# Shifts of a 32-head attention kernel in pieces on GpSimd, wherever VectorE's plan has room; a fuller TensorE tick

## The chip, the cores and the metric

The kernel runs on one core of one Trainium2 chip. Its metric is the device time of a launch in microseconds (us), the median of some runs. A core has five engines with queues of their own: TensorE (PE in the profile) multiplies matrices into PSUM, ScalarE (ACT) and VectorE (DVE) work on SBUF and PSUM, GpSimd (POOL) works on SBUF, and SyncE (SP) here issues the DMAs. Every engine takes its instructions in the order in which the program emits them, and waits at an instruction for semaphores that others raise.

## The reference

It is attention with normalised queries and keys, for 32 heads of 2048 positions and 20 features, in bf16:

```
qn = q / (jnp.sqrt((q * q).sum(axis=-1, keepdims=True)) + eps)
kn = k / (jnp.sqrt((k * k).sum(axis=-1, keepdims=True)) + eps)
logits = jnp.einsum('bhqd,bhkd->bhqk', qn, kn) * t[None, :, None, None]
attn = _softmax(logits, axis=-1)
return jnp.einsum('bhqk,bhkd->bhqd', attn, v)
```

Each head has 2048 x 2048 logits, and each logit needs an exponential: 134 million in all. The logits of normalised vectors times a temperature near 1 are small, so no maximum is taken off.

## The kernel before, in words

**Two ways to an exponential.** The keys of a head are cut into 16 row blocks of 128, the queries into four groups of 512 columns. A block against a group is a unit, a PSUM bank of 128 x 512. For most blocks ScalarE computes the exponential of the scores from PSUM (psA) into a ring in SBUF (p_ring), in waves of two and three units in turn (line 785). TensorE multiplies it with the values (vaug, which has a column of ones for the softmax's denominator) into psO (line 714). For the other blocks VectorE does it: `DVE_TILES` (line 378) says how many blocks of each head, 4 to 6. For such a block, a *tile* of four units, VectorE reads the scores from PSUM (psD) in two instructions of 1024 columns, multiplies and adds, and writes int16 (xt, line 831): the bits of an fp16 number near the exponential, whose mantissa is linear in the logit. To smooth this out, three *shifts* follow, each an addition of 256, 512 or 768 (`PHASES`) to the int16 numbers, into tiles ss (line 851). TensorE multiplies xt with vaug and each of the three shifted tiles with values scaled by the matching power of two (vph), and so adds up four approximations.

**Shifts on GpSimd.** `KDN` (line 386) says for each head how many tiles have their third shift (`PSH` = 2) done by GpSimd: two pieces of `PCH` = 512 words each, a word being two int16 numbers that are added as one int32 (line 857). In all 99 shifts, 198 pieces. GpSimd also scales values (vph, line 522), normalises queries and keys of heads 3 and later (qkn, line 589) and divides the output (o_stage, line 738).

**Preparation.** For each head q and k are loaded into qk_sb (one buffer a head, 8 in turn), VectorE squares them (sq, line 554) and sums 32 rows of 20 (rs_sum, line 556); six small instructions make the inverse root (lines 559 to 577). Heads 0, 1 and 2 are prepared alone, then heads in pairs: squares and sums for each head, the small instructions for both. A transposing DMA and ten more bring the result into the layouts of TensorE (qkT, qz, kR).

**The plan.** The order of all engines comes from a planner in the kernel (`Program`, lines 44 to 340), which runs while the program is built. Each piece of work is a `Task` with an engine, a duration, dependences and a priority (a due time in heads). `list_schedule` plays the engines forward and lets each take the ready task with the least priority. It writes down the order; the semaphore waits follow from it. For GpSimd there is `pool_fill` (line 182): whenever VectorE is given an instruction that reads PSUM or reduces (names t1, tr, su), it is the *span* under which GpSimd's instructions are to lie, and a task of GpSimd that has a length `win` is placed there if it ends at most `OVER` = 0.03 us after the span. It then gets an extra dependence, its *trigger*: the instruction of VectorE just before, or the one before that. So GpSimd starts with the read and not in the middle of a shift.

`schedule` repeats that plan in passes. Score matmuls can run with 32, 64 or 128 rows of the array (`modes`; the score of 20 features fits in 32), and matmuls of fewer rows run beside each other. After each pass it adds up the TensorE columns that end in each stretch of `TICK` = 3.41 us, each task by its weight, and where the sum is under `LOAD` = 3500 it moves score matmuls to more rows (heavy), and takes some back where there are many more.

**Buffers.** xt has `NX` = 4 buffers, each ss `NE` = 3. A buffer is used again when its readers are done.

Of the kernel before, what the change touches and what calls it, by code (L numbers as in the profile page):

```python
# [9 lines left out]
BF16 = mybir.dt.bfloat16  # L10
FP16 = mybir.dt.float16
# [19 lines left out]
class Task:  # L31
    __slots__ = ("eng", "fn", "dur", "deps", "pri", "name", "lat", "dma", "n", "users",
                 "start", "end", "seq", "inc", "cnt", "rows", "work", "modes", "win", "trig")

    def __init__(self, eng, name, fn, dur, deps, pri, lat=0.0, dma=None):
        self.eng, self.name, self.fn, self.dur = eng, name, fn, dur
        self.deps = [d for d in deps if d is not None]
        self.pri, self.lat, self.dma = pri, lat, dma
        self.inc, self.cnt = False, 0
        self.rows, self.work, self.modes = 128, 512.0, None  # L40
        self.win, self.trig = 0.0, None


class Program:
# [3 lines left out]
    SEM_LAT = {"PE": 0.20, "ACT": 0.17, "DVE": 0.14, "POOL": 0.15, "SP": 0.0}  # L48

    SWITCH = 0.5  # L50
    LIGHT = 9.0
    TICK = 3.41
    LOAD = 3500.0
    PASSES = 12
    FIRM = 4
    MARGIN = 300.0
# [3 lines left out]
    SPARE = 0.0  # L60
    DSL = 0.6
    HOLDA = 0.7
    HPE = 0.1
    HDV = 0.08
# [11 lines left out]
    def schedule(self):  # L76
# [49 lines left out]
        self.heavy = heavy  # L126
        for t in self.tasks:
            if t.trig is not None:
                t.deps.append(t.trig)
        return self.order  # L130

    def list_schedule(self):
        for t in self.tasks:
            t.users = []
            t.trig = None
        for i, t in enumerate(self.tasks):
# [45 lines left out]
        def pool_fill(now):  # L182

            n = 0
            while True:
# [9 lines left out]
                fit = [r for r in ready["POOL"] if r[2].win and at + r[2].win <= span[1] + self.OVER]  # L195
                if not fit:
                    return n
                x = min(fit)
                ready["POOL"].remove(x)
                heapq.heapify(ready["POOL"])  # L200
                t = x[2]
# [6 lines left out]
                leave(t, now)  # L208
                n += 1
# [133 lines left out]
def bass_standalone__qk_norm__prompt_kernel(  # L343
# [16 lines left out]
    NB = 8  # L360
# [3 lines left out]
    NX = 4  # L364
    NE = 3
    GD = 1
# [5 lines left out]
    SPREAD = 0.8  # L372
    FIRST = -7.0
    DLEAD = 0.8
# [3 lines left out]
    DVE_TILES = [4, 4, 4, 5, 5, 5, 5, 5, 4, 5, 5, 5, 5, 4, 5, 5, 5, 5, 5, 5, 4, 5, 5, 5, 5, 6, 5, 5, 5, 4, 4, 6]  # L378
    NDMAX = 6
    NPOOL, FPOOL = True, True  # L380
    SQPOOL = False
# [4 lines left out]
    KDN = (4, 5, 2, 4, 3, 2, 4, 4, 2, 2, 4, 3, 3, 3, 4, 2, 4, 3, 3, 4, 3, 3, 5, 2, 3, 5, 2, 4, 2, 3, 3, 2)  # L386
    ADUR, ALAT = 0.95, 6.5
    PSH = 2
    ASTEP, AOFF = 2, 0
    ACCN = (0, 0, 0, 0, 0, 0, 0, 0, 0, 0, 0, 0, 0, 0, 0, 0, 0, 0, 0, 0, 0, 0, 0, 0, 0, 0, 0, 0, 0, 0, 0, 0)  # L390
    NLAST = 1
    PCH, PRATE = 512, 0.00164
    SHP = 0.0

    with ExitStack() as es:  # L395
# [7 lines left out]
        two = sbuf("two", [128, 1], I32)  # L403
        cst = sbuf("cst", [128, 2048], I16)
        ident = sbuf("ident", [128, 128], BF16)
        qk_sb = [sbuf(f"qk_sb{i}", [128, 2 * R, D], BF16) for i in range(NB)]
        vaug = [sbuf(f"vaug{i}", [128, R, 32], BF16) for i in range(NV)]
        vph = [sbuf(f"vph{i}", [128, len(PHASES), NDMAX, 32], FP16) for i in range(NV)]
        sqs = [sbuf(f"sq{i}", [128, 2 * R, D], BF16) for i in range(2)]
        rs = {x: sbuf(f"rs_{x}", [128, 4 * R], F32) for x in ("sum", "u", "a", "b", "y", "r")}  # L410
# [6 lines left out]
        xt = [sbuf(f"xt{i}", [128, GD * 2048], I16) for i in range(NX)]  # L417
        ss = [[sbuf(f"ss{j}_{i}", [128, GD * 2048], I16) for i in range(NE)] for j in range(len(PHASES))]
# [14 lines left out]
        def memset(eng, ap, val, dur, pri):  # L433
            return add(eng, "z", lambda e, tk: e.memset(ap, val), dur, pri=pri)
# [24 lines left out]
        D_groups = [list(range(i, min(i + GD, len(D_tiles)))) for i in range(0, len(D_tiles), GD)]  # L459
# [10 lines left out]
        memset("POOL", two[:, :].bitcast(I16), PHASES[PSH], 0.1, -98)  # L470
        z_cst = memset("POOL", cst[:, :], PHASES[2], 0.3, -70)
# [22 lines left out]
        last_sum = []  # L494
# [3 lines left out]

        def add_loads(h):
            b, bv = h % NB, h % NV  # L500
            pri = h - LEAD - 0.5
            war = (norm[h - NB] if h >= NB else []) + ([lambda: [trn[max(0, h - 4)]]] if h >= EARLY else [])
            x = qk_sb[b]
# [24 lines left out]
        def add_prep(hs):  # L528
# [16 lines left out]
            for i, h in enumerate(hs):  # L545
                x = qk_sb[h % NB]
                sqb = sqs[h % 2]
                if SQPOOL and h > 2:
                    m = 2 * R // NCH
                    s1 = [pool("sq", lambda e, tk, x=x, sqb=sqb, j=j: e.tensor_tensor(  # L550
                        sqb[:, j:j + m, :], x[:, j:j + m, :], x[:, j:j + m, :], ALU.mult),
                        m * D * TTRATE, lds[h] + last_sum[-2:-1]) for j in range(0, 2 * R, m)]
                else:
                    s1 = [dv("sq", lambda e, tk, x=x, sqb=sqb: e.tensor_tensor(sqb[:, :, :], x[:, :, :], x[:, :, :], ALU.mult),  # L554
                          0.41, lds[h] + last_sum[-2:-1] + (q0[2:] if h == 1 else []))]
                sums.append(dv("sum", lambda e, tk, i=i, sqb=sqb: e.tensor_reduce(  # L556
                    rs["sum"][:, 2 * R * i:2 * R * (i + 1)], sqb[:, :, :], AXIS_X, ALU.add), 0.73, s1 + prep_last[0]))
                last_sum.append(sums[-1])
            c = dv("rs", lambda e, tk: e.tensor_scalar(  # L559
                rs["u"][:, 0:w].bitcast(I32), rs["sum"][:, 0:w].bitcast(I32), -0.5, RS_MAGIC, ALU.mult, ALU.add),  # L560
                0.075 + 0.03 * n, sums)
# [20 lines left out]
            for i, h in enumerate(hs):  # L582
                x, b = qk_sb[h % NB], h % NN
                war = [trn[h - NN]] + (q0 if h == NN else []) if h >= NN else [z_qkn[b]]
                if NPOOL and h > 2:
                    norm[h] = []
                    m = 2 * R // NCH
                    for j in range(0, 2 * R, m):
# [3 lines left out]
                            m * D * TTRATE + 0.25, [c] + war, due + SPREAD)  # L592
# [32 lines left out]
        def first_head(rinv):  # L625
            x = qk_sb[0]
# [128 lines left out]
        def add_wave(w):  # L755
# [24 lines left out]
            for h in hs:  # L780
# [6 lines left out]
                0.0633 + n / 1200.0, qks + war, w)  # L787
# [13 lines left out]
        dusers = {}  # L801

        def add_dgroup(jg):
            js = D_groups[jg]
            sx, se = jg % NX, jg % NE
            w = 2048 * len(js)
            old = lambda n, ring: dusers.get((n, jg - ring), [])
            t1s = []
            for i, j in enumerate(js):
# [3 lines left out]
                for k in range(0, NG, n1):  # L813
# [11 lines left out]
                    for g in gs:  # L825
# [4 lines left out]
                    o = 2048 * i + 512 * k  # L830
                    t1_prev[nchunk[0]] = add("DVE", f"t1.{j}.{k}", lambda e, tk, o=o, slot=slot: e.tensor_scalar(  # L831
                        xt[sx][:, o:o + W1], psD[:, slot * W1:slot * W1 + W1], X_MUL, X_ADD, ALU.mult, ALU.add),
                        0.067 + W1 / 960.0, [qk] + old("x", NX), due - 5)
                    t1s.append(t1_prev[nchunk[0]])
            x = xt[sx][:, 0:w]

            def dv(name, fn, dur, deps):
                return add("DVE", f"{name}{js[0]}", fn, 0.068 + dur * len(js), deps, due)
            sh = []
            h0, n0 = D_tiles[js[0]][0], js[0] - d0[D_tiles[js[0]][0]]  # L840
            nd0 = DVE_TILES[h0]
            order = [(n * ASTEP + AOFF) % nd0 if math.gcd(ASTEP, nd0) == 1 else n for n in range(nd0)]
            kind = order.index(n0)
            by_dma = jg >= 2 and h0 < H - NLAST and kind < ACCN[h0]
            by_pool = jg >= 2 and not by_dma and kind < ACCN[h0] + KDN[h0]
            for i in range(len(PHASES)):
                dst, war = ss[i][se], t1s + old(f"s{i}", NE)
                if i == 2 and by_dma:
                    sh.append(None)
                elif i != PSH or not by_pool:  # L850
                    sh.append([dv(f"s{i}.", lambda e, tk, i=i, dst=dst: e.tensor_scalar(  # L851
                        dst[:, 0:w], x, float(PHASES[i]), None, ALU.add), 0.533, war)])
                else:
                    sh.append([])
                    for c in range(0, w // 2, PCH):
                        n = min(PCH, w // 2 - c)
# [98 lines left out]
```

## Time and profile before

| | |
|---|---|
| Median of 3 runs | 665.07 us (664.13 to 665.85) |
| The profiled execution, its own time | 664.62 us |
| Its span, first to last instruction | 662.8 us |
| Granted TensorE clock, mean | 1.000 |
| GpSimd (POOL) | 369.7 us busy, 375 instructions |
| DMA, mean over the span | 55 GB/s |

The span is what the profile's sums are made against; 1.8 us of the execution lie around it. A row of the groups gives a line and an engine, the operation, what is written and read, the shape and the count; behind the bar stand busy time and the mean length of a record in ns; behind the second bar the idle time of the engine before these instructions, with what ended it. Records of ScalarE and VectorE reach over the start of the next instruction, by 0.08 to 0.09 us on VectorE, so that the length of a record is not the time for which its engine's queue is held. From the order in time this is seen as the distance from start to start.

### The profile page before, as it was taken

How to read it: one execution, taken by the hardware profiler on the slowest of the kernel's cores; microseconds unless marked ns; L12 is line 12 of the kernel's file. 1: busy time of each engine (PE TensorE's matmuls, PEld its weight loads, DVE VectorE, ACT ScalarE, POOL GpSimd, SP SyncE). 2: the span in 40 equal slices, each digit the busy share in tenths (PEclk: the TensorE clock that was granted, in tenths of full speed). 3: DMA queues.
4: the chain of work that ended last, by engine and by line, in shares of the span. 5: the costliest groups of instructions: out<-in, count | busy, mean ns of one | idle time of the engine just before them, and what ended most of it. 6: DMA issues, size and time to landing. Idle time of an engine off the chain costs nothing.

```text
span 662.8 us, 14627 instructions
## 1 busy us (share of the span) xinstructions
PE 579.4 (87%) x5949; PEld 163.2 (25%) x5971; DVE 655.2 (99%) x927; ACT 655.1 (99%) x582; POOL 369.7 (56%) x375
## 2 busy tenths in 40 slices
PE   7787989988898888898889898888989889988997
PEld 2222222222222222222222222222222222222222
DVE  9999999999999999999999999999999999999997
ACT  8999999999999999999999999999999999999997
POOL 3346565565654456655666556565675664554550
PEclk9999999999999999999999999999999999999999
DMA  5454524243242432513435250353514224032200
GB/s 64 64 80 81 66 43 80 30 74 48 53 75 31 82 35 59 70 20 84 43 73 65 48 80 10 75 62 65 67 28 79 37 53 73 3 77 35 54 7 11
DMA packets 196723, 36.24 MB, mean 55 GB/s; under 512 B 172592, under 2 KB 196656, under 8 KB 196656
## 3 DMA queue, kind: packets, MB, share of 16 engines
q1 hardware_dynamic: 196512, 35.22, 34.0%
q8 instruction: 47, 0.77, 0.5%
q14 instruction: 20, 0.16, 0.1%
q10 hardware_dynamic: 144, 0.08, 0.1%
HBM read 7.87 MB, written 2.62 MB: 16 GB/s over the span
## 4 chain that ended last, share of the span: by engine, by line
ACT 91%; DVE 6%; DMA 1%; issue 1%; PE 0%; SPq 0%; ACTq 0%
ACT p_ring L785 91%; DVE xt L831 3%; DVE ss L851 1%; DMA qkT<-qkn 1%; DVE rs_sum L556 0%; DMA qk_sb<-in_k_dram 0%; DVE rs_u L559 0%; DMA qz<-qkT 0%; DVE sq L554 0%; SPq L431 0%; DVE qz L665 0%; DVE oT L727 0%; ACTq L395 0%; DVE kx L673 0%; DVE o_stage L738 0%
## 5 line engine op out<-in xcount | busy, mean ns | idle before, releaser
L785 ACT ACTIVATE p_ring<-psA 128x1024 bf16<-128x1024 f32 (+1 forms) x573 | 647.7, 1402 | 1.5 <-PE psA L694 1.5
L831 DVE TENSOR_SCALAR xt<-psD 128x1024 int16<-128x1024 f32 x308 | 374.9, 1217 | 1.7 <-PE psD L694 0.7
L857 POOL TENSOR_TENSOR ss<-xt,two 128x512 int32<-128x512 int32 x198 | 250.8, 1267 | 171.6 <-DVE ss L851 79.5
L694 PE MATMUL psA<-qz,kR 32*128 32x512 bf16 (+2 forms) x1063 | 217.5, 385 | 47.0 <-ACT p_ring L785 42.4
L851 DVE TENSOR_SCALAR ss<-xt 128x2048 int16<-128x2048 int16 x363 | 243.2, 688 | 0.0
L714 PE MATMUL psO<-ss,vph 128*32 128x512 f16 x1848 | 171.2, 385 | 0.7 <-POOL ss L857 0.7
L714 PE MATMUL psO<-p_ring,vaug 128*32 128x512 bf16 x1432 | 132.2, 385 | 0.7 <-ACT p_ring L785 0.7
L694 PE MATMUL psA<-qz,qkT 32*128 32x512 bf16 (+2 forms) x354 | 115.4, 384 | 15.0 <-ACT p_ring L785 13.4
L694 PE MATMUL psD<-qz,kR 64*128 64x512 bf16 (+1 forms) x456 | 118.5, 385 | 9.5 <-DVE xt L831 6.5
L694 PEld LDWEIGHTS psA<-qz,kR 32*128 32x128 bf16 (+2 forms) x1074 | 52.9, 92 | 183.1 <-ACT p_ring L785 179.7
L522 POOL TENSOR_SCALAR vph<-vaug 128x160 f16<-128x160 bf16 (+2 forms) x96 | 37.1, 386 | 48.9 <-DVE ss L851 22.5
L589 POOL TENSOR_TENSOR qkn<-qk_sb,rs_r 128x640 bf16<-128x640 bf16 x29 | 47.8, 1647 | 28.0 <-DVE ss L851 13.6
L714 PEld LDWEIGHTS psO<-ss,vph 128*32 128x32 f16 x1848 | 44.4, 94 | 73.1 <-issue 56.1
L694 PE MATMUL psD<-qz,qkT 64*128 64x512 bf16 (+1 forms) x153 | 57.6, 385 | 3.8 <-DVE xt L831 3.3
L714 PE MATMUL psO<-xt,vaug 128*32 128x512 f16 x616 | 59.9, 384 | 0.0
L714 PEld LDWEIGHTS psO<-p_ring,vaug 128*32 128x32 bf16 x1432 | 35.0, 94 | 54.9 <-issue 46.0
L738 POOL TENSOR_TENSOR o_stage<-oT,rec 128x320 bf16<-128x320 f32 x30 | 29.3, 978 | 33.3 <-DVE rec L730 15.8
L694 PEld LDWEIGHTS psD<-qz,kR 64*128 64x128 bf16 (+1 forms) x462 | 28.9, 93 | 71.5 <-DVE xt L831 57.2
L694 PEld LDWEIGHTS psA<-qz,qkT 64*128 64x128 bf16 (+2 forms) x358 | 28.0, 92 | 61.7 <-ACT p_ring L785 59.6
L556 DVE TENSOR_REDUCE rs_sum<-sq 128x32 f32<-128x640 bf16 x32 | 26.0, 812 | 0.1
L727 DVE STREAM_TRANSPOSE oT<-psO 128x512 f32<-128x512 f32 x32 | 22.7, 709 | 2.0 <-PE psO L714 2.0
L714 PEld LDWEIGHTS psO<-xt,vaug 128*32 128x32 bf16 x616 | 15.9, 94 | 23.1 <-issue 19.2
(47 smaller groups left out, 92.0 us busy)
## 6 DMA issues: line engine op xcount, KB each, us to landing
kR<-qkT SPq DMA_DIRECT2D x62, 96.0 KB, 2.2
qz<-qkT SPq DMA_DIRECT2D x124, 32.0 KB, 1.8
kR<-qkT SPq DMA_DIRECT2D x62, 64.0 KB, 2.0
qk_sb<-in_k_dram SPq DMA_DIRECT2D x32, 80.0 KB, 2.5
vaug<-in_v_dram SPq DMA_DIRECT2D x32, 80.0 KB, 3.6
qk_sb<-in_q_dram SPq DMA_DIRECT2D x124, 20.0 KB, 2.6
out_dram<-o_stage SPq DMA_DIRECT2D x31, 80.0 KB, 2.3
kR<-qkT SPq DMA_DIRECT2D x62, 32.0 KB, 1.9
```

Source lines behind the costliest of these rows:

```text
L522: vsc[h] = [add("POOL", f"vs{h}", lambda e, tk, i=i: e.tensor_scalar(vph[bv][:, i, 0:nd, :], vaug[bv][:, R - nd:R, :], 2.0 ** (-PHASES[i] ...
L556: sums.append(dv("sum", lambda e, tk, i=i, sqb=sqb: e.tensor_reduce(rs["sum"][:, 2 * R * i:2 * R * (i + 1)], sqb[:, :, :], AXIS_X, ALU.add ...
L589: u = add("POOL", f"norm{h}", lambda e, tk, x=x, b=b, i=i, j=j: e.tensor_tensor(qkn[b][:, j:j + m, 0:D], x[:, j:j + m, :], bc(rs["r"][:, 2 ...
L694: return eng.matmul(dst, lhsT, mov, tile_position=(p0, 0))
L714: last = eng.matmul(psO[32 * g:32 * g + 32, :], w, rhs_of(g), start=start, stop=False, skip_group_check=True, tile_position=(0, 32 * g))
L727: trO[h] = add("DVE", f"tr{h}", lambda e, tk: e.transpose(oT[:, :, :].rearrange("p r d -> p (r d)"), psO[:, :]), 0.63, [lambda: pv_users[h ...
L738: fin[h] = add("POOL" if pool else "DVE", f"fin{h}", lambda e, tk: e.tensor_tensor(st, src, rb, ALU.mult), TTDUR if pool else 0.40, [rc] + ...
L785: act[w] = add("ACT", f"exp{w}", lambda e, tk: e.activation(p_ring[:, p0 * 512:p0 * 512 + n], psA[:, slot * WAVES[0] * 512:slot * WAVES[0] ...
L831: t1_prev[nchunk[0]] = add("DVE", f"t1.{j}.{k}", lambda e, tk, o=o, slot=slot: e.tensor_scalar(xt[sx][:, o:o + W1], psD[:, slot * W1:slot ...
L851: sh.append([dv(f"s{i}.", lambda e, tk, i=i, dst=dst: e.tensor_scalar(dst[:, 0:w], x, float(PHASES[i]), None, ALU.add), 0.533, war)])
L857: u = add("POOL", f"s{i}.{js[0]}.{c}", lambda e, tk, i=i, dst=dst, c=c, n=n: e.tensor_tensor(dst[:, 2 * c:2 * (c + n)].bitcast(I32), xt[sx ...
```

## The change

The shifts that go to GpSimd are no longer listed by head. Every shift of a tile (but those of the first two) is a VectorE task that also has a form for GpSimd, `alt`. When `pool_fill` finds no other task of GpSimd that fits, it takes the last-due shift from VectorE's ready ones, if VectorE has at least `KEEP` = 0.3 us of other work ready, and cuts off as many words as fit into what is left of the span, at least 128, in steps of 32. The rest waits for the next span. Such a shift becomes GpSimd's for good; its matmuls wait for all its pieces.

```diff
+    PRATE = 0.00164
+    KEEP = 0.3
+    RESTP = 0.3
...
+    def piece(self, words, fixed=0.02):
+        return fixed + words * self.PRATE
...
-                fit = [r for r in ready["POOL"] if r[2].win and at + r[2].win <= span[1] + self.OVER]
-                if not fit:
-                    return n
...
+                room = span[1] + self.OVER - at
+                fit = [r for r in ready["POOL"] if r[2].win and r[2].win <= room]
+                if fit:
...
+                else:
+                    cand = [r for r in ready["DVE"] if r[2].alt]
+                    if not cand or self.piece(128) > room or sum(r[2].dur for r in ready["DVE"]) < self.KEEP + cand[0][2].dur:
+                        return n
+                    x = max(cand)
+                    ready["DVE"].remove(x)
...
+                    t.parent, t.rem, t.seq = x[2], 1024, x[2].seq
+                    t.parent.eng = "POOL"
+                rest = None
+                if t.parent:
+                    f = t.parent
+                    m = min(t.rem, max(128, int((room - self.piece(0)) / self.piece(1, 0.0)) // 32 * 32))
+                    if 0 < t.rem - m < 128:
+                        m = t.rem - 128
+                    if t.rem > m:
+                        rest = Task("POOL", f.name, None, 0.0, [], t.pri)
...
+                f = add("DVE", f"s{i}.{js[0]}", lambda e, tk, i=i, dst=dst: e.tensor_scalar(
+                    dst[:, be:be + w], xt[0][:, bx:bx + w], float(PHASES[i]), None, ALU.add), 0.068 + w / 3840.0,
+                    t1s + [u for m in range(len(js)) for u in old(f"s{i}", m)], due)
+                if len(js) == 1 and jg >= 2:
+                    f.alt = lambda c, n, i=i, dst=dst: lambda e, tk: e.tensor_tensor(
```

In the same diff the preparation changes. From head 3 on GpSimd folds the squares, the first ten features of each row added to the last ten (fold, in fp32), and VectorE sums what is left; heads 5 and later come in pairs with one square and one sum for both, heads 3 and 4 singly. For this qk_sb is one tensor.

```diff
-        preps = [[h] for h in range(min(NSOLO, H))] + [list(range(h, min(h + 2, H))) for h in range(NSOLO, H, 2)]
+        preps = [[h] for h in range(min(NSOLO, H))] + [[3], [4]] + [list(range(h, min(h + NQ, H))) for h in range(NSOLO + 2, H, NQ)]
...
+            parts = [(i, min(2, n - i)) for i in range(0, n, 2)] if FUSE and hs[0] > 2 else [(i, 1) for i in range(n)]
...
+                        c2.append(pool("fold", lambda e, tk, a=a, k=k, at=at: e.tensor_tensor(
+                            at[k + 1][0][:, a:a + 2 * R, :], at[k][0][:, a:a + 2 * R, 0:at[k + 1][1]],
+                            at[k][0][:, a:a + 2 * R, at[k + 1][1]:2 * at[k + 1][1]], ALU.add),
```

The constants change too. `LOAD`, the columns asked of each tick, goes up with the room kept when some are taken back; the planner's delays are set anew; the rings grow; and the tiles are spread differently over the heads, 157 for 154 in all.

```diff
-    SEM_LAT = {"PE": 0.20, "ACT": 0.17, "DVE": 0.14, "POOL": 0.15, "SP": 0.0}
-
-    SWITCH = 0.5
+    SEM_LAT = {"PE": 0.20, "ACT": 0.30, "DVE": 0.14, "POOL": 0.15, "SP": 0.0}
+
+    SWITCH = 0.1
...
-    LOAD = 3500.0
-    PASSES = 12
-    FIRM = 4
-    MARGIN = 300.0
+    LOAD = 3550.0
+    PASSES = 16
+    FIRM = 8
+    MARGIN = 600.0
...
-    NX = 4
-    NE = 3
-    GD = 1
+    NX = 6
+    NE = 4
...
-    DVE_TILES = [4, 4, 4, 5, 5, 5, 5, 5, 4, 5, 5, 5, 5, 4, 5, 5, 5, 5, 5, 5, 4, 5, 5, 5, 5, 6, 5, 5, 5, 4, 4, 6]
+    DVE_TILES = [4, 4, 4, 5, 4, 5, 5, 5, 5, 5, 5, 5, 5, 5, 6, 5, 6, 5, 5, 5, 5, 3, 5, 5, 5, 4, 5, 6, 6, 5, 5, 5]
```

## The prediction

> **What bounds the kernel now.** I read the busy totals first, then the chain of waits, then the groups with shapes kept apart, then the order in time.
>
> ```profile
> PE 579.4 (87%) x5949; PEld 163.2 (25%) x5971; DVE 655.2 (99%) x927; ACT 655.1 (99%) x582; POOL 369.7 (56%) x375
> ...
> PEclk9999999999999999999999999999999999999999
> ...
> ACT 91%; DVE 6%; DMA 1%; issue 1%; PE 0%; SPq 0%; ACTq 0%
> ...
> 54.99 602.71 ACT p_ring L785 x533
> ```
>
> Two engines are full, but the chain names one: from 55 us to 657.7 us it runs through 533 exponentials on ScalarE with nothing between them. VectorE is the co-bound: 99% busy, and hardly idle before any of its work.
>
> ```profile
> L785 ACT ACTIVATE p_ring<-psA 128x1536 bf16<-128x1536 f32 x286 | 461.2, 1613 | 1.5 <-PE psA L694 1.5
> L831 DVE TENSOR_SCALAR xt<-psD 128x1024 int16<-128x1024 f32 x308 | 374.9, 1217 | 1.7 <-PE psD L694 0.7
> L785 ACT ACTIVATE p_ring<-psA 128x1024 bf16<-128x1024 f32 x287 | 342.1, 1192 | 0.0
> L857 POOL TENSOR_TENSOR ss<-xt,two 128x512 int32<-128x512 int32 x198 | 250.8, 1267 | 171.6 <-DVE ss L851 79.5 <-DVE xt L831 30.2 <-DVE sq L554 12.4
> L851 DVE TENSOR_SCALAR ss<-xt 128x2048 int16<-128x2048 int16 x363 | 243.2, 688 | 0.0
> ```
>
> Records of one engine overlap, so the mean of a record is not what an instruction costs its queue. I use the distance from start to start: in the order in time three shifts start at 296.07 and the next read at 297.87, so **a shift costs 0.60 us**; reads at 294.94 and the shift after it at 296.07 give **1.13 us a PSUM read**, 0.09 under its record. For ScalarE the chain gives 602.71 / 533 = 1.131 us per exponential; the two shapes differ by (1613 - 1192) = 421 ns, so 1.34 us for 1536 columns and 0.92 us for 1024. The engine's records start the first exponential at 9.39 us and end the last at 658.6 us. Its 649 us hold about 640 us of bare work (286 x 1.330 + 287 x 0.904, the median distances) and 9 us of small stalls.
>
> **ScalarE's part.** DVE_TILES sums to 154 before and 157 after. A tile is four units of 512 columns, so 12 units leave ScalarE. Counted in the two programs, 286 wide and 287 narrow exponentials become 284 and 284: 2 x 1.34 + 3 x 0.92 = **-5.4 us**, all on the chain.
>
> **VectorE's part**, at start-to-start distances:
> - Three more tiles: 6 more reads x 1.134 = +6.8 us.
> - Shifts kept on VectorE: 363 to 352 (157 x 3 = 471, less 119 that GpSimd takes; before 99). 11 x 0.60 = -6.6 us.
> - Row sums. Before, 32 reductions of 640 elements at 0.73 (start to start; record 812 ns) = 23.3 us. After, three stay as they are (2.2), three read a folded half (0.065 + 320 / 960 = 0.40 each, 1.2), and 13 take two folded heads at once, again 640 elements, 0.73 each (9.5): 12.9 us, so -10.4 us.
> - Squares: 32 x 0.40 = 12.8 us become 6 x 0.40 + 13 x 0.73 = 11.9 us, -0.9 us. Only the shared start (0.065) is saved.
> - One more set of the small root instructions, since heads 3 and 4 are prepared singly: +0.4 us.
>
> Sum: **-10.7 us**. VectorE's work at median distances is 650.5 us now, so about 640 us after, against 634 + 9 us on ScalarE. ScalarE stays the end; VectorE's reserve grows by 10.7 - 5.4 = 5.3 us. That reserve covers what is uncertain below.
>
> **GpSimd's part.** 198 pieces of 512 words become 334 pieces of 128 to 672 words (59 of 672, 49 of 160, 51 of 192, 29 of 128), 121,856 words for 101,376, and 29 folds come in. GpSimd is 56% busy, with waits for VectorE inside that. Does a piece fit under its read?
>
> ```profile
> 249.77 1.42 POOL L857 TENSOR_TENSOR ss<-xt,two 128x512 int32<-128x512 int32 x1 [4.83 <-DVE rs_r L571]
> 252.21 1.65 POOL L589 TENSOR_TENSOR qkn<-qk_sb,rs_r 128x640 bf16<-128x640 bf16 x1 [1.02 <-DVE ss L851]
> ...
> 249.61 0.69 DVE L851 TENSOR_SCALAR ss<-xt 128x2048 int16<-128x2048 int16 x1
> 250.21 1.22 DVE L831 TENSOR_SCALAR xt<-psD 128x1024 int16<-128x1024 f32 x1
> ...
> 252.64 1.23 DVE L831 TENSOR_SCALAR xt<-psD 128x1024 int16<-128x1024 f32 x1
> 253.78 0.69 DVE L851 TENSOR_SCALAR ss<-xt 128x2048 int16<-128x2048 int16 x1
> ...
> 561.94 0.77 DVE L851 TENSOR_SCALAR ss<-xt 128x2048 int16<-128x2048 int16 x1
> ```
>
> A 512-word piece with nothing in its way has a record of 1.04 us (that at 293.13). Here it starts under a shift, takes 1.42 and ends at 251.19: it stood still for 0.38 us, until the read was about to begin, and ended 0.15 us before the next VectorE instruction (251.34). The 640-element norm does the same, ends at 253.86, **0.08 us after** the next shift began (253.78), and that shift is no longer than others (0.69, next start 0.59 later). The shift at 561.94 began 0.22 us before a GpSimd piece ended (561.12 plus 1.04); its record is 0.77, 0.09 over the usual. So about 0.13 us of overrun is free, and beyond that it costs its own length.
>
> A 672-word piece is not in the trace. From the norm (1.27 net for 640) and o_stage (0.73 for 320) a word costs 1.7 ns, so 1.04 + 160 x 1.7 ns = 1.31 us, an overrun of some 0.12 us: just inside what is free. Bounds: 0 and 0.04 us x 59 = 2.4 us on VectorE; I take 0, since the norm is nearest. Small pieces: bounds 0 (a 160-element vph scaling, 0.32 us, sits under reads unnoticed) and 0.09 us, the one measured block, for each of 334, 30 us. I take 0, because the plan gives each piece only what is left of its read; the upper end is the rival on the slow side.
>
> **A rule that speaks against it.** The Trainium skill, "GPSIMD Engine Reference", section 4.1 "Engine selection", says to keep elementwise adds off GpSimd, about twice as slow for two inputs; its section 3.1 gives 4497 ns for 2048 elements, 2.2 ns each. By that figure 121,856 words would be 268 us, and planned at 1.64 ns a word they would overrun their reads by 68 us in all, mostly out of VectorE's time: well above 700 us. The row says 1.04 us for 512 with start included, 1.7 ns a word at the margin, and the slow add costs nothing while VectorE reads PSUM beside it. I go by the row.
>
> **TensorE.** Counted in the two programs, 98 matmuls into psA run at full height (128 rows) for 66 before: 16 more narrow waves, whose two matmuls then follow one another, some 0.2 us more each, +3.2 us of TensorE. A tile on VectorE has four output passes for one, so three tiles add 36 output matmuls, nine groups of four at 0.4 us or less. TensorE is 87% busy. By the 33 full-height waves of before, ScalarE is on average 7 ns late, less than after the light forms (10 to 23 ns), so I cost this at 0; if TensorE had no slack it would be 16 x 0.2 = 3 us. The Trainium skill, "TensorE: Matmul & The Clock Gate", Part 1, has the clock halve after about 3.4 us of too little activity. By that rule a fuller tick could gain; by the row the granted clock is full in all 40 slices, so there is nothing to get back, and I take 0.
>
> **New waits.** A row sum now waits for a fold on GpSimd, with everything on VectorE behind it. The fold is placed about three heads ahead of its use, and other VectorE work stands between; cost 0, at most one late fold of 0.73 us x 16. Shift matmuls wait for a last piece; behind them on TensorE stand the scores that ScalarE needs. Before, TensorE's loads waited for GpSimd twice, 1.2 us in all. Twice as many pieces: 0 to 2.4 us; I take 0. The rings xt and ss grow from 4 and 3 to 6 and 4 buffers, which eases it. Head 3's and 4's loads go later in SP's queue by one head; the start (to 55 us, where ScalarE lost about 2 us) may move by 1 us either way.
>
> **The sum.** 664.62 us of the profiled execution (span 662.8, 1.8 around it) less 5.4 is 659.2; against the median of 665.07 it is 659.7. I say **659.5 us**, 0.8% faster.
>
> **Rivals.**
> - *VectorE's reserve also clears ScalarE's stalls.* Of the 9 us some 7 are stalls of 0.1 to 0.3 us spread over the run. Half of them gone: 656. For: VectorE less full. Against: they follow TensorE's queue, which gets fuller. 0.14.
> - *Late pieces stall TensorE's queue.* Each of 119 GpSimd shifts holding it 0.05 us gives the 5.4 back: 664.5. 0.09.
> - *Pieces block VectorE (slower).* Place: the shift that follows a read with a piece under it. Price: the 0.09 us seen at 561.94. From 10.7 / 334 = 0.032 us a piece on, VectorE is as full as today and the kernel turns slower; at two pieces of three (223 x 0.09 = 20 us) it is 650.5 - 10.7 + 20 = 660 us of VectorE work, 9 over today: 674. For: the largest pieces stand at the edge. Against: 198 pieces and 29 norms almost never blocked. 0.15.
> - The forecast, 657 to 663: 0.62.
>
> A measurement of this kernel tells about 0.3% (2 us) from no change. The cases give faster 0.78, same 0.07, slower 0.15. The range from 655 to 666.5 leaves the blocked case out.
>
> **What would show it.** Right: the unbroken run of exponentials about 5 us shorter (597 us for 602.71), shifts still 0.60 us start to start, VectorE's share a point or two lower. Wrong: shift records well over 0.69 after reads with a 672-word piece; VectorE at 99% with longer records; "POOL ss" as the releaser of TensorE loads with more than a few us; a granted clock under 1.

## The result and the profile after

| | before | after |
|---|---|---|
| Median, measured side by side | 664.98 us (664.13 to 665.85, 4 runs) | 661.5 us (660.44 to 662.2, 4 runs) |
| Ratio, 95% interval | | 0.9946 [0.9926, 0.9967] |
| The profiled execution, its own time | 664.62 us | 662.08 us |
| Its span | 662.8 us | 660.4 us |
| Granted TensorE clock, mean | 1.000 | 0.995 |

The change makes the kernel 0.5% faster, 3.5 us. That is less than the 0.8% forecast, and more than the 0.3% that can be told from nothing. The page after has these busy totals, clock slices and shares of the chain of waits:

```profile
PE 591.1 (90%) x5979; PEld 168.0 (25%) x6007; DVE 645.3 (98%) x902; ACT 649.7 (98%) x577; POOL 469.2 (71%) x542
...
PEclk9999899999999999999999999999999999999999
...
ACT 81%; DVE 14%; PE 2%; SPq 1%; issue 1%; DMA 1%; POOL 0%; DVEq 0%
```

Three things are to be seen. GpSimd went from 56% to 71% busy, and VectorE from 655.2 us to 645.3 us: the work moved. ScalarE lost only 5.4 us of records and still is what the run ends with. And two places are new: the fifth clock slice (66 to 82.5 us) is under 9, where before all 40 were full, and the chain is on ScalarE for 81% instead of 91%: after the stretch described below it runs through VectorE, and the last unbroken run of exponentials begins only at 123.63 us:

```profile
123.63 532.56 ACT p_ring L849 x471
```

The groups, all shapes of a line together (busy and mean record in ns, then the idle time ahead and what ended it):

```profile
L849 ACT ACTIVATE p_ring<-psA 128x1024 bf16<-128x1024 f32 (+1 forms) x568 | 642.5, 1433 | 5.1 <-PE psA L758 5.0
L916 POOL TENSOR_TENSOR ss<-xt,add_w 128x672 int32<-128x672 int32 (+14 forms) x335 | 322.5, 969 | 110.5 <-DVE ss L912 58.0
L905 DVE TENSOR_SCALAR xt<-psD 128x1024 int16<-128x1024 f32 x314 | 381.9, 1216 | 9.2 <-PE psD L758 7.9
L912 DVE TENSOR_SCALAR ss<-xt 128x2048 int16<-128x2048 int16 x352 | 234.5, 681 | 0.3
```

The shift records are 681 ns for 688 before, so the pieces under the reads do not lengthen them. But ScalarE now waits 5.1 us for TensorE's scores where it waited 1.5 us, and VectorE 9.2 us before its reads where it waited 1.7 us. The list of waits says that it is not many small ones:

```profile
DVE xt L905 <- PE psD L758: 7.9, 11, 3.2
ACT p_ring L849 <- PE psA L758: 5.0, 5, 2.8
PEld psD L758 <- DMA kR<-qkT: 3.5, 1, 3.5
PE psD L758 <- DMA kR<-qkT: 3.0, 1, 3.0
```

Sum, times, longest: five waits make ScalarE's 5.0 us, one of them 2.8 us long, and TensorE waited once, for 3.0 us, for a DMA that writes kR, the rotated keys of a head.

Where the 2.4 us of span went, from the distances start to start: the bare work of ScalarE fell from 639.8 to 634.5 us (-5.3, with 284 wide at 1.330 and 284 narrow at 0.904); the first exponential starts at 8.66 us for 9.39 (-0.7); the stalls between exponentials grew from 9.1 to 12.8 us (+3.8); the tail is 4.2 us both times. This gives -2.2. Of the 12.8 us of stalls, **5.6 us lie between 61 and 70 us** (3.2, 1.04, 0.30 and 1.06 over the bare distances).

The order in time there, ScalarE first, then SP's queue:

```profile
54.57 8.44 ACT L849 ACTIVATE p_ring<-psA 128x1536 bf16<-128x1536 f32 x7
65.81 1.02 ACT L849 ACTIVATE p_ring<-psA 128x1024 bf16<-128x1024 f32 x1 [2.80 <-PE psA L758]
67.75 1.45 ACT L849 ACTIVATE p_ring<-psA 128x1536 bf16<-128x1536 f32 x1 [0.92 <-PE psA L758]
69.38 1.02 ACT L849 ACTIVATE p_ring<-psA 128x1024 bf16<-128x1024 f32 x1 [0.18 <-PE psA L758]
```

```profile
45.46 3.37 SPq L473 DMA_DIRECT2D qk_sb<-in_q_dram  x4
48.88 0.63 SPq L473 DMA_DIRECT2D qk_sb<-in_k_dram  x1
49.55 1.26 SPq L473 DMA_DIRECT2D qk_sb<-in_q_dram  x2
50.85 1.37 SPq L671 DMA_TRANSPOSE qkT<-qkn  x1
52.27 2.00 SPq L473 DMA_DIRECT2D out_dram<-o_stage  x4
54.30 0.62 SPq L473 DMA_DIRECT2D qk_sb<-in_q_dram  x1
54.97 2.53 SPq L473 DMA_DIRECT2D qz<-qkT  x4
57.54 3.77 SPq L473 DMA_DIRECT2D kR<-qkT  x6
```

The norm of head 3 was done at 47.65 us, but its transposition was issued at 50.85: SP was still issuing the loads of heads 5 and 6. Its kR copies were issued one after the other up to 60.72. The chain of waits carries on from there (start, length):

```profile
60.72 3.97 DMA kR<-qkT
64.73 0.61 PE psD L758 x2
```

The last copy landed at 64.7, 4.0 us after its issue, where the rest took 1.8 to 2.2. TensorE's queue stood at the psD scores of head 3 from 61.7 us on, and behind them stood the scores for ScalarE. In the kernel before, TensorE came to these scores at 67.53, and the last kR copy, issued at 63.58, had landed at 65.77 (SP's queue, then TensorE):

```profile
60.02 4.24 SPq L431 DMA_DIRECT2D kR<-qkT  x6
67.53 0.39 PE L694 MATMUL psD<-qz,kR 64*128 64x512 bf16 x2
```

So the new plan uses head 3 some 6 us sooner, and issues its last copy only 2.9 us sooner. A rough estimate of the parts: with the 2.1 us of flight that the others had, the copy would have landed at about 62.8 and held TensorE for 1.1 us; the other 1.9 us of its 3.0 us of waiting are the longer flight.

The same stretch as windows (window, its length, busy time and count of PE, PEld, DVE, ACT, POOL, then granted clock, DMA share, GB/s):

```profile
60.00:62.00 2.00, 1.74 (x27) 0.43 (x19) 2.00 (x7) 2.00 (x3) 0.00 (x0) 1.00 0.43 93
62.00:65.00 3.00, 0.27 (x2) 0.13 (x4) 0.13 (x1) 1.01 (x1) 1.09 (x1) 0.87 0.60 61
65.00:70.00 5.00, 5.00 (x35) 0.86 (x31) 3.54 (x4) 3.09 (x3) 2.06 (x2) 0.50 0.57 53
```

TensorE had 0.27 us of work in 3 us, and in the 5 us after that its **granted clock was 0.50**: matmuls of 0.61 instead of 0.39 us, and TensorE full while ScalarE waited for it three more times. Two windows set to the stretch of the slow clock show that it is 6.8 us long:

```profile
60.80:64.20 3.40, 0.94 (x15) 0.22 (x11) 1.33 (x5) 2.21 (x2) 1.09 (x1) 1.00 0.65 83
64.20:71.00 6.80, 6.27 (x40) 1.21 (x40) 3.76 (x5) 3.50 (x3) 2.89 (x4) 0.50 0.58 66
```

The wait for the late copy cost ScalarE 3.2 us, the three stalls after it another 2.4 us. How much of the 2.4 is the slow clock and how much is work left over from the standstill is not separated by any run.

### The profile page after: what moved, and what is told of

It reads as the page before. It is cut to its first block, busy times and chain, and to the rows that moved or that the text cites. A ratio compares the mean times of both kernels' runs of the same rounds, so it can differ in the third digit from the quotient of the medians.

```text
span 660.4 us, 14800 instructions
## 1 busy us (share of the span) xinstructions
PE 591.1 (90%) x5979; PEld 168.0 (25%) x6007; DVE 645.3 (98%) x902; ACT 649.7 (98%) x577; POOL 469.2 (71%) x542
## 4 chain that ended last, share of the span: by engine, by line
ACT 81%; DVE 14%; PE 2%; SPq 1%; issue 1%; DMA 1%; POOL 0%; DVEq 0%
ACT p_ring L849 81%; DVE xt L905 7%; DVE ss L912 4%; SPq L473 1%; PE psO L685 1%; DMA kR<-qkT 1%; DVE rs_sum L619 1%; PE psO L778 1%; DVE sq L604 0%; DVE oT L791 0%; PE psD L758 0%; PE psA L758 0%; DVE qkn L660 0%; DVE qz L729 0%; DVE o_stage L802 0%
## 5 line engine op out<-in xcount | busy, mean ns | idle before, releaser
L916 POOL TENSOR_TENSOR ss<-xt,add_w 128x672 int32<-128x672 int32 (+14 forms) x335 | 322.5, 969 | 110.5 <-DVE ss L912 58.0
L905 DVE TENSOR_SCALAR xt<-psD 128x1024 int16<-128x1024 f32 x314 | 381.9, 1216 | 9.2 <-PE psD L758 7.9
L912 DVE TENSOR_SCALAR ss<-xt 128x2048 int16<-128x2048 int16 x352 | 234.5, 681 | 0.3
L778 PE MATMUL psO<-ss,vph 128*32 128x512 f16 x1884 | 166.6, 386 | 0.0
L758 PE MATMUL psD<-qz,kR 64*128 64x512 bf16 (+1 forms) x466 | 121.0, 386 | 8.7 <-DVE xt L905 4.8
L778 PE MATMUL psO<-p_ring,vaug 128*32 128x512 bf16 x1420 | 124.3, 386 | 0.1
L574 POOL TENSOR_SCALAR vph<-vaug 128x160 f16<-128x160 bf16 (+3 forms) x96 | 40.6, 423 | 32.5 <-DMA vaug<-in_v_dram 13.1
L758 PEld LDWEIGHTS psA<-qz,qkT 32*128 32x128 bf16 (+2 forms) x355 | 27.9, 92 | 55.6 <-ACT p_ring L849 54.3
L612 POOL TENSOR_TENSOR fold<-sq 128x320 f32<-128x320 bf16 x29 | 28.5, 982 | 9.4 <-DVE ss L912 5.8
```

The lines of the kernel that those rows point to most:

```text
L574: vsc[h] = [add("POOL", f"vs{h}", lambda e, tk, i=i: e.tensor_scalar(vph[bv][:, i, 0:nd, :], vaug[bv][:, R - nd:R, :], 2.0 ** (-PHASES[i] ...
L612: c2.append(pool("fold", lambda e, tk, a=a, k=k, at=at: e.tensor_tensor(at[k + 1][0][:, a:a + 2 * R, :], at[k][0][:, a:a + 2 * R, 0:at[k + ...
L758: return eng.matmul(dst, lhsT, mov, tile_position=(p0, 0))
L778: last = eng.matmul(psO[32 * g:32 * g + 32, :], w, rhs_of(g), start=start, stop=False, skip_group_check=True, tile_position=(0, 32 * g))
L912: f = add("DVE", f"s{i}.{js[0]}", lambda e, tk, i=i, dst=dst: e.tensor_scalar(dst[:, be:be + w], xt[0][:, bx:bx + w], float(PHASES[i]), No ...
L916: f.alt = lambda c, n, i=i, dst=dst: lambda e, tk: e.tensor_tensor(dst[:, be + 2 * c:be + 2 * (c + n)].bitcast(I32), xt[0][:, bx + 2 * c:b ...
```

## The experiments

My theory after the result: the planned work came in as summed, and the start lost 5.6 us to the late kR copies of head 3 (theory A in most of the expectations below). The rival: what was lost lies in the body, in pieces that block VectorE, in GpSimd's folds or in TensorE's fuller queue. Each edit below is made on the changed kernel; "H6" is the edit of the first experiment. Any edit makes the planner lay out everything anew, so single stalls come and go from one to the next; that counts in what follows.

**1. Head 6's loads wait for head 3's transposition (H6).** In the loads, the transposition that a head's load waits for:

```diff
-            war = (norm[h - NB] if h >= NB else []) + ([lambda: [trn[max(h - 3, 0) if h < 5 else h - 4]]] if h >= EARLY else [])
+            war = (norm[h - NB] if h >= NB else []) + ([lambda: [trn[max(h - 3, 0) if h < 5 else 3 if h == 6 else h - 4]]] if h >= EARLY else [])
```

> One trigger moved: head 6's loads of q and k wait for head 3's transposition instead of head 2's, so that SP issues head 3's transposition three loads (about 2 us) earlier. Theory A: the changed kernel lost about 5.6 us of ScalarE time between 61 and 70 us because the last kR transfer of head 3 landed at 64.7 us, after TensorE stood at it, and the granted clock then fell. Then this run is at 656 to 658 us (ratio about 0.988), with no ScalarE gap over 1 us after 55 us and a clock of 1.000. Theory B: the stall only moves to another wait of the start, or comes from a transfer that is slow whenever it is issued. Then 660 to 662 us (ratio 0.993 to 0.996).

Measured: 657.41 us (657.23 to 658.12), before 664.75, ratio 0.9893 [0.9879, 0.9906]; twice the gain of the change. The order in time, SP and ScalarE:

```profile
50.30 1.36 SPq L671 DMA_TRANSPOSE qkT<-qkn  x1
51.71 2.00 SPq L473 DMA_DIRECT2D out_dram<-o_stage  x4
53.75 2.50 SPq L473 DMA_DIRECT2D qz<-qkT  x4
56.29 3.78 SPq L473 DMA_DIRECT2D kR<-qkT  x6
```

```profile
48.92 14.89 ACT L849 ACTIVATE p_ring<-psA 128x1024 bf16<-128x1024 f32 x13
64.09 11.53 ACT L849 ACTIVATE p_ring<-psA 128x1536 bf16<-128x1536 f32 x10 [0.28 <-PE psA L758]
```

The transposition came only 0.55 us sooner, less than expected. But the q load that stood between it and the kR copies is gone, these went out 1.25 us sooner, and the last one took 2.1 us and landed at 61.61. ScalarE runs through with 0.9 us of stalls at 61 to 65 us for 5.6, and the clock stays full there:

```profile
62.00:65.00 3.00, 3.00 (x39) 0.98 (x41) 2.60 (x5) 2.71 (x3) 2.14 (x2) 1.00 0.59 58
65.00:70.00 5.00, 4.63 (x50) 1.27 (x48) 5.00 (x7) 4.99 (x5) 3.94 (x7) 1.00 0.49 42
```

Over the run ScalarE's stalls are 8.6 us, less than the 9.1 of before. So it is shown that the loss in the start came with the late copy, and the body gives up nothing. The place in the queue is the smaller part of it, though: the last copy landed 3.07 us sooner, of which 1.24 us are its earlier issue and 1.84 us its shorter flight. This version beats both kernels.

**2. The old spread of tiles (154) in the changed kernel.** `DVE_TILES` from before; the rest of the change stays, the stall in the start too.

```diff
-    DVE_TILES = [4, 4, 4, 5, 4, 5, 5, 5, 5, 5, 5, 5, 5, 5, 6, 5, 6, 5, 5, 5, 5, 3, 5, 5, 5, 4, 5, 6, 6, 5, 5, 5]
+    DVE_TILES = [4, 4, 4, 5, 5, 5, 5, 5, 4, 5, 5, 5, 5, 4, 5, 5, 5, 5, 5, 5, 4, 5, 5, 5, 5, 6, 5, 5, 5, 4, 4, 6]
```

> The list of tiles by head is that of the kernel before (154 tiles), all else as in the changed kernel; 12 units go back to ScalarE. Theory A: ScalarE sets the end, so 2 x 1.330 + 3 x 0.904 = 5.4 us come back: 666 to 668 us if the stall at 61 us stays (ratio 1.002 to 1.005), 661 to 663 if it goes. The other parts of the change (pieces, fold, tick) gain nothing by themselves. Theory B: a lighter VectorE pays by itself, because ScalarE's small stalls (9 us before) come from it: under 660 us.

Measured: 667.36 us (666.25 to 667.7), ratio 1.0036 [1.0023, 1.0048]: slower than before, and 5.9 us over the changed kernel, whose 12 units fewer were summed at 5.4.

```profile
PE 597.9 (90%) x5971; PEld 164.6 (25%) x5971; DVE 635.3 (95%) x891; ACT 655.0 (98%) x582; POOL 457.3 (69%) x535
```

VectorE is down to 95%, and the time does not fall. The pieces, the folds and the rings mainly make room; the time comes from the tiles put into the room. The stall at 61 us is here unchanged (3.05, 1.04, 0.30 and 1.04 us). Its span is 2.8 us over that of before; less these 5.4 us it would be some 2.6 us under it (an estimate), of which 0.9 us is an earlier first exponential. So a small gain without the tiles is not excluded.

**3. Three more tiles (160) over H6.** Heads 4, 21 and 25 get one more each.

```diff
-    DVE_TILES = [4, 4, 4, 5, 4, 5, 5, 5, 5, 5, 5, 5, 5, 5, 6, 5, 6, 5, 5, 5, 5, 3, 5, 5, 5, 4, 5, 6, 6, 5, 5, 5]
+    DVE_TILES = [4, 4, 4, 5, 5, 5, 5, 5, 5, 5, 5, 5, 5, 5, 6, 5, 6, 5, 5, 5, 5, 4, 5, 5, 5, 5, 5, 6, 6, 5, 5, 5]
```

> As the run with head 6's loads later, and three more tiles (160): heads 4, 21 and 25 get one each. ScalarE: 281 wide, 282 narrow and one single exponential, 629 us of bare work, 5.3 less. VectorE: 6 reads and 8 shifts more, about 11.6 us, some 652 us of work, as full as before the change. Theory A: ScalarE still sets the end, its stalls stay near 9 us: 651 to 654 us (ratio 0.981). Theory B: VectorE is full again and holds ScalarE up: 656 us or more.

Measured: 668.3 us (667.96 to 669.76), ratio 1.0059 [1.0047, 1.0072]. Theory B held: VectorE is full. Its bare work is 651.7 us (637.7 with H6 alone). Two windows at the end:

```profile
600.00:655.00 55.00, 51.06 (x517) 14.37 (x518) 53.80 (x71) 55.00 (x50) 28.96 (x30) 1.00 0.09 20
655.00:668.00 13.00, 7.62 (x80) 1.92 (x70) 9.89 (x14) 0.41 (x1) 2.81 (x3) 0.76 0.02 7
```

ScalarE has its last exponential behind it at 655.4 us and VectorE goes on until 663.6. With H6 alone ScalarE ended at 651.7 and VectorE's last shift at 647.5. Between 154 and 160 tiles the end passes from one engine to the other.

**4. No shift on GpSimd, over H6.**

```diff
-                if len(js) == 1 and jg >= 2:
+                if False:
```

> As the run with head 6's loads later, and GpSimd takes no shift; all 471 stay on VectorE, 122 more, 73 us of work. Theory A: VectorE, at about 640 us of work, becomes the bound: 640 + 73 = 713 us and its small waits, 715 to 725 us. Theory B: the matmuls that no longer wait for pieces and the free GpSimd give much back: under 705 us.

Measured: one run of 721.58 us beside 664.44 of before.

```profile
PE 615.1 (85%) x5963; PEld 173.7 (24%) x6007; DVE 711.7 (99%) x1021; ACT 652.1 (91%) x577; POOL 145.7 (20%) x207
```

As theory A has it: VectorE's bare work of 711.6 us is the time, ScalarE is at 91%. GpSimd's slow adds carry 64 us of this kernel against H6.

**5. Pieces that run over their read, over H6.** The planner lets a piece end 0.25 us after its span instead of 0.03, and makes them that much longer.

```diff
-    OVER = 0.03
+    OVER = 0.25
```

> As the run with head 6's loads later, with OVER, by which the plan lets a piece end after its read, at 0.25 us instead of 0.03: pieces up to 800 words (35 of them), 136 shifts on GpSimd, 335 on VectorE (14 fewer, 8.4 us less). Theory A: overrun is free up to about 0.13 us and then costs its own length: the shifts after full pieces get longer by about 0.2 us, some 150 pieces, 25 to 30 us of VectorE's time; 665 to 680 us (ratio 1.00 to 1.02). Theory B: GpSimd's end records run on after it has left the port, so that the overrun stays free: 656 to 658 us, with shift records as before.

Measured: 686.01 us (685.19 to 686.68), ratio 1.0309 [1.0289, 1.0329], above the range of theory A. One piece of the changed kernel, GpSimd and then VectorE:

```profile
211.75 1.69 POOL L916 TENSOR_TENSOR ss<-xt,add_w 128x672 int32<-128x672 int32 x1 [0.73 <-DVE ss L912]
...
212.19 1.22 DVE L905 TENSOR_SCALAR xt<-psD 128x1024 int16<-128x1024 f32 x1
213.32 1.28 DVE L912 TENSOR_SCALAR ss<-xt 128x2048 int16<-128x2048 int16 x2
```

It ends at 213.44, 0.12 us after the next shift began, and the two shifts take 1.28 us, as two do with no piece over them (0.60 + 0.68). One of this experiment:

```profile
92.94 1.90 POOL L916 TENSOR_TENSOR ss<-xt,add_w 128x800 int32<-128x800 int32 x1 [0.73 <-DVE ss L912]
...
93.38 1.22 DVE L905 TENSOR_SCALAR xt<-psD 128x1024 int16<-128x1024 f32 x1
94.52 1.48 DVE L912 TENSOR_SCALAR ss<-xt 128x2048 int16<-128x2048 int16 x2
```

It reaches 0.32 us into the shift, and the two take 1.48 us: +0.20. Over all such cases: 21 pieces of 672 words in the changed kernel overlap a shift by 0.11 us (median) and add nothing to its record; here 640-word pieces mostly overlap by 0.28 and add 0.15, 800-word pieces by 0.325 and add 0.19, and the few between, at 0.19 us, add 0.06. The blocking was rightly described and its size rightly guessed, but the lengthened records add up to some 7 us only. The rest of the 28 us is waits between the engines that follow (idle time ahead of ScalarE's and VectorE's work):

```profile
L849 ACT ACTIVATE p_ring<-psA 128x1024 bf16<-128x1024 f32 (+1 forms) x568 | 643.2, 1402 | 20.0 <-PE psO L778 18.4 <-PE psA L758 1.4
L905 DVE TENSOR_SCALAR xt<-psD 128x1024 int16<-128x1024 f32 x314 | 382.5, 1218 | 24.2 <-PE psD L758 20.1
```

ScalarE stands 18.4 us behind output matmuls of TensorE, in 8 waits, and VectorE 20.1 us behind its scores, in 59. How a late shift comes to hold each of them was not followed further.

**6. Pieces of 512 words at most, over H6.**

```diff
-                    m = min(t.rem, max(128, int((room - self.piece(0)) / self.piece(1, 0.0)) // 32 * 32))
+                    m = min(t.rem, 512, max(128, int((room - self.piece(0)) / self.piece(1, 0.0)) // 32 * 32))
```

> As the run with head 6's loads later, and no piece is over 512 words, so that none ends after its read: 316 pieces, 110 shifts on GpSimd instead of 122; 12 more on VectorE, 7.2 us. Theory A: the 672-word pieces, which end about 0.11 us after the next VectorE instruction has begun, block nothing, so the cap gains nothing; VectorE has the 7 us to spare or nearly: 657 to 660 us (ratio 0.989 to 0.993). Theory B: the overrun costs VectorE something that its records do not show; then the cap is faster than 657 us in spite of fewer shifts.

Measured: 660.34 us (659.6 to 662.84), ratio 0.9929 [0.991, 0.9947]. GpSimd takes 110 shifts in 316 pieces for 122 in 336 with H6 alone, and VectorE's bare work is 645.6 us for 637.7. The time is 2.9 us over H6 and just above the range of theory A, and nothing is seen of a harm done by the large pieces (theory B). That they gain is not shown: other runs over H6 lie up to 2.5 us above it, and this trace has stalls of 1.3, 0.4 and 0.6 us at 74 to 78 us beside a granted clock of 0.50 from 74.7 to 78.1.

Its start shows the two parts of the late copy apart. H6 is in it, but the planner laid the start out anew: here head 3's kR copies went out 0.76 us later than in the changed kernel, the last at 61.48 us:

```profile
58.30 3.77 SPq L473 DMA_DIRECT2D kR<-qkT  x6
64.46 8.41 ACT L849 ACTIVATE p_ring<-psA 128x1536 bf16<-128x1536 f32 x7 [0.45 <-PE psA L758]
```

That copy took 2.1 us and landed at 63.61. TensorE came to the scores of head 3 at 63.02 (61.74 in the changed kernel) and stood still for 0.68 us, ScalarE lost 0.75 us, and the clock stayed full there. Here a copy that was issued late and landed in the usual time cost little.

**7. No folds on GpSimd** (in the changed kernel, without H6).

```diff
-    FUSE, FOLD = True, 1
+    FUSE, FOLD = True, 0
```

> The fold of the squares on GpSimd is left out; VectorE sums all 20 features again, pairs of heads stay fused. In its plan GpSimd takes 135 shifts instead of 119, and head 3's transposition is issued before the loads of heads 5 and 6. Theory A: fold and shift compete for the same GpSimd time, and what counts is only that VectorE stays below ScalarE: VectorE gets about 10 us more of sums and 16 x 0.60 = 9.6 us fewer shifts, so the time is that of the changed kernel without its stall at 61 us, 656 to 659 us. Theory B: the fold is what makes VectorE's reserve; without it VectorE holds ScalarE up, 663 us or more.

Measured: 659.53 us (658.38 to 660.39), ratio 0.992 [0.9906, 0.9933]. GpSimd fills its freed time with shifts, 135 for 119, so that VectorE's bare work is 640.7 us for 640.3: fold and shift trade one for one. The 2 us under the changed kernel stand beside a transposition of head 3 that went out at 43.47 us instead of 50.85; the stall of 61 us is not there, only one of 1.2 us ahead of the exponential at 67.2. This run found a second way around it without aiming at it.

**8. The old tick over H6.**

```diff
-    LOAD = 3550.0
-    PASSES = 16
-    FIRM = 8
-    MARGIN = 600.0
+    LOAD = 3500.0
+    PASSES = 12
+    FIRM = 4
+    MARGIN = 300.0
```

> As the run with head 6's loads later, with the tick of the kernel before: 3500 columns, margin 300, 12 passes, the last 4 without taking back. Theory A: the tick of the change neither gains nor costs, since the granted clock is full either way: 656.5 to 658.5 us, clock as in that run. Theory B: fuller ticks keep the clock up; then the clock falls in some stretch and the time is 660 us or more. Theory C: fewer full-height matmuls give ScalarE an earlier start of its waves: under 656 us.

Measured: 658.92 us (658.26 to 659.24), ratio 0.99 [0.9884, 0.9916]. Its trace has 41 full-height waves for 54 with H6, a full clock outside the tail, and one stall of 1.4 us at 427 us, which is about its distance from H6. It lies between the theories. The fuller tick brings no clock, since none was missing; a small effect either way is left open.

**9. The last head with 6 tiles (158), over H6.**

```diff
-    DVE_TILES = [4, 4, 4, 5, 4, 5, 5, 5, 5, 5, 5, 5, 5, 5, 6, 5, 6, 5, 5, 5, 5, 3, 5, 5, 5, 4, 5, 6, 6, 5, 5, 5]
+    DVE_TILES = [4, 4, 4, 5, 4, 5, 5, 5, 5, 5, 5, 5, 5, 5, 6, 5, 6, 5, 5, 5, 5, 3, 5, 5, 5, 4, 5, 6, 6, 5, 5, 6]
```

> As the run with head 6's loads later, and a sixth tile in the last head (158 in all), where VectorE stood idle for 4.9 us before the last transposition. ScalarE has 1.8 us less. Theory A: VectorE's 3 to 4 us more fit into that idle time: 655.5 to 656.5 us (ratio about 0.987). Theory B: VectorE now ends the last head later than ScalarE would: 657 us or more.

Measured: 657.65 us (656.65 to 659.0), ratio 0.9883 [0.9865, 0.9901], not to be told from H6. VectorE now does its last shift at 652.7 us, after ScalarE's last exponential at 651.5: as theory B has it, the end passes to VectorE, and one tile more gains nothing. Its trace also has stalls of 1.2 and 0.6 us at 279 to 283, beside a granted clock of 0.50 from 279.4 to 282.8, so that a gain of under 2 us could be hidden.

**10. GpSimd may take only the third shift of a tile, over H6.** This limits which matmuls can wait for a late piece.

```diff
-                if len(js) == 1 and jg >= 2:
+                if len(js) == 1 and jg >= 2 and i == 2:
```

> As the run with head 6's loads later, but only the third shift of a tile (768) may go to GpSimd, in pieces as before; GpSimd gets 118 shifts instead of 122, VectorE 353 (4 more, 2.4 us). Theory A: how many words fit under the reads counts, not which shift it is; VectorE has the 2.4 us to spare: 656.5 to 659 us. Theory B: that any shift may go is what fills GpSimd at the right moments; then VectorE waits or stands full: 661 us or more.

Measured: 659.9 us (659.34 to 660.41), ratio 0.9925 [0.9905, 0.9945], between the theories, so it decides nothing. A kR copy landed late again (issued 60.75, landed 64.59 us) and cost 1.6 us at 63 to 66; two more stalls of 1.5 and 1.4 us lie at 388 and 429.

**What stays open.** The runs over H6 that should have equalled it lie 1.5 to 3 us above it, each with single stalls of 1.4 to 1.7 us at other places. Which rule of the planner makes those was not settled. Nor was why the last kR copy takes 4 us. In the three traces where it does (the changed kernel, experiments 2 and 10), an instruction fetch, a packet of 16 KB on a queue of its own, begins between 61.8 and 62.0 us, while the copy is under way. In experiment 1 the fetch came at 62.8, after the copy had landed; in experiment 6 none came between 58 and 64, and the copy was not late.

This is more than one coincidence. The twelve traces of this case hold 2232 kR copies. Of the 1850 that no such packet overlapped, 2 took over 3 us (3.03 and 3.09); of the 382 that one overlapped, 123 did, up to 4.2 us. The late ones landed 1.0 to 2.4 us after the packet had ended. So a late kR copy goes with an instruction fetch almost without exception, and about one copy in three that meets a fetch is late. What joins them was not tested: no run moved a fetch by itself.

## Why the prediction was right, and where it was not

- **Forecast and direction.** 661.5 us lies inside the range, and 2 us above the 659.5 named: 3.5 us gained of about 5.5. Two terms that the sum put at nothing stand between them, with opposite signs: stalls of ScalarE (+3.8 us) and an earlier first exponential (-0.7). The sign named for being right, an unbroken run of exponentials of about 597 us, did not come.
- **ScalarE's -5.4 us.** Right: -5.3 us of bare work, and 5.9 us between the old and the new spread of tiles in the same kernel.
- **VectorE's -10.7 us.** Right: 650.5 to 640.3, so -10.2. The reserve that was to cover the uncertain parts was there, and experiment 3 shows that its end is real: three tiles more and VectorE sets the end.
- **The pieces.** Right at the edge where they stood: 1.31 us was estimated for 672 words, 1.300 was measured with nothing in the way; "about 0.13 us of overrun is free" held on 21 pieces, and the price beyond it, "its own length", on the two sizes of experiment 5. Row against rule, the row was right: 128 to 672 words take 0.39 to 1.30 us, 0.18 us and 1.67 ns a word, not the 2.2 ns an element of the Trainium skill's "GPSIMD Engine Reference", section 3.1; and without this work on GpSimd the kernel takes 721.6 us.
- **TensorE's fuller waves at 0.** Right: after 49 full-height waves ScalarE was late by 5 ns on average, against 7 after the 33 of before.
- **Waits for pieces at 0.** Right. The list of waits of the changed kernel has one row for it, and none for a fold:

```profile
PEld psO L778 <- POOL ss L916: 0.5, 2, 0.2
```

- **What failed: the start.** The step said that "Head 3's and 4's loads go later in SP's queue by one head; the start (to 55 us, where ScalarE lost about 2 us) may move by 1 us either way". The sizes in it are wrong. What was late was not the loads of head 3 but its last kR copy, in part because its transposition stood behind the loads of heads 5 and 6 on the same queue, and for the larger part because it took 4.0 us to land; and it struck after the 55 us, where the run of exponentials before had no gap. It cost 5.6 us. The flight of a copy was no term of the sum. That this one met an instruction fetch is a matter of the layout, so part of the loss is bad luck, and part of experiment 1's gain is good luck. With the copies in time (experiment 1) 4.7 us of that went, and the time fell by 4.1 us to 657.4, 2 us under the forecast. Of that 2 us about 1 us is an earlier first exponential (8.43 us for 9.39), which was not in the sum.
- **The clock at 0.** In the body of this kernel that was right. But the sum had taken "there is nothing to get back" for "there is nothing to lose": one standstill of 3 us brought a half clock for 6.8 us. The signs named had it ("a granted clock under 1"), the sum did not. The Trainium skill's "TensorE: Matmul & The Clock Gate", Part 1, has the clock halve after an idle window of about 3.4 us. In this trace it halved 2.5 us after TensorE's last matmul had ended, with 0.94 us of work in the 3.4 us before. In experiment 3 it halved at 443.2 us with no standstill over 0.52 us in the 3.4 us before, in which TensorE was busy for 2.18 us:

```profile
439.80:443.20 3.40, 2.18 (x16) 0.51 (x14) 3.40 (x6) 3.40 (x5) 2.43 (x4) 1.00 0.53 51
443.20:446.60 3.40, 3.33 (x19) 0.62 (x23) 2.30 (x3) 2.47 (x4) 3.04 (x5) 0.50 0.08 24
```

So an idle stretch of that length is not needed here; thin work was enough. Stretches of 3.4 us at half clock also lie in the body of experiments 4, 5 and 9.

## What to carry to other kernels

Two nearly full engines leave room to move work, but time comes only from the work that leaves the last one: here freed VectorE time was worth little until tiles were put in it, and three tiles too many made it the end. When a plan pulls a stage forward, follow every DMA that feeds it through its queue, issue by issue, with what is issued ahead of it, and leave room for one that takes twice as long to land as its like (here 125 of 2232 took over 3 us where most took about 2); the price of being late is the wait and, on TensorE, the risk of a slow clock after it. Filling an engine's gaps with pieces cut to size costs nothing up to a sharp edge, so measure where that edge lies before choosing how far to go.

## What was not expected of the hardware

- A GpSimd piece may end about 0.13 us after VectorE's next shift began and costs it nothing (0.11 us over: nothing, 21 cases). From there each part of a microsecond counts in full: 0.19 over costs 0.06, 0.28 over costs 0.15, 0.325 over costs 0.19.
- One standstill of TensorE of 3.0 us was followed by 6.8 us at a granted clock of 0.50, and the stalls of ScalarE in that time (2.4 us) came near to the wait itself (3.2 us). In experiment 3 the clock halved with no standstill over 0.52 us.
- Copies of the same size from the same queue landed 2.1 us or 4.0 us after their issue in one trace, and the late one was the one waited for. In all traces, 123 of the 125 kR copies that took over 3 us had a 16 KB instruction fetch under way beside them.
